# V of the first four token tiles from x as loaded, in a linear attention and SwiGLU kernel on Trainium2

## The chip, the cores and the metric

The kernel runs on one core of one Trainium2 chip. A core has a matrix engine (TensorE, PE in the profile), a vector engine (VectorE, DVE), a scalar engine for activations (ScalarE, ACT), a general engine (GpSimd, POOL) and a queue engine (SyncE, SP) that issues the transfers between DRAM and the core's memory here. [...] Each engine takes its instructions in the order of the program and waits on semaphores. The metric is the device time of one launch, in microseconds (us).

## What is computed

The input x has 2048 tokens of 640 numbers. It is normalised per token (mean and variance, no weights) to xn, and two branches of xn are added to x: a linear attention of 32 heads with a Hedgehog feature map, and a SwiGLU block with 1536 hidden columns.

```python
xn = _layernorm(x, axis=-1)
# A: q, k, v = split(xn @ wqkv), 32 heads of 20
pq = einsum("bhsd,hdf->bhsf", q, w_phi); pk = einsum("bhsd,hdf->bhsf", k, w_phi)
phi_q = concat([softmax(pq), softmax(-pq)]); phi_k = concat([softmax(pk), softmax(-pk)])
kv = einsum("bhsf,bhsd->bhfd", phi_k, v); z = einsum("bhsf->bhf", phi_k)
o = einsum("bhqf,bhfd->bhqd", phi_q, kv) / (einsum("bhqf,bhf->bhq", phi_q, z) + 1e-6)
a = o.reshape(B, S, D) @ wo
# B
b = (silu(xn @ w1) * (xn @ w3)) @ w2
return x + a + b
```

## The kernel before

The tokens are cut into 16 tiles of 128. `xin` holds x tiles as loaded (three buffers of four tiles, inside `reg_h`), `xnT` the normalised tiles transposed, `wv` the V weights (a third of `reg_w`), `wkT` and `wqT` the transposed K and Q weights (the other two thirds). The program is written out by hand in the order that each engine is to follow (`manual_schedule`), so a line's place in the code is its place in its engine's queue.

- **Loads.** SP issues all transfers (`ld`, L117; `ldT`, L130; transposes of `xnT`, L278). First x tiles 0 and 1, `wv` in three pieces (row blocks 0, 1 to 2, 3 to 4), x tiles 2 and 3. Two small POOL copies (L644, L649) hold the next loads back: columns 0 to 256 of w1 and w3, then x tiles 4 to 11, columns 256 to 512 of w1 and w3, and w_phi. x tiles 12 to 15 go to the buffer of tiles 0 to 3 (L677).
- **Warming.** 44 matmuls of zeros (`WARM`, `warm`, L193) run on PE while the first tile is loaded and normalised.
- **Normalising.** Per tile: statistics on DVE (`ln_stats`, L214 and L217), the root on ACT for tiles 0 to 3 (`ln_root`, L233), reciprocal and normalisation in place on DVE (`lx`, L616 and L268). For tiles 4 to 15 the inverse root is made on POOL (`stats`, L225 to L253).
- **Transposing.** `x_transposed` (called `T`) brings a normalised tile into `xnT`: tiles 0 to 3 by five PE transposes into PSUM (L282) and two ACT copies (L286), tiles 4 to 15 (`BY_DMA = 4`) by a DMA transpose (L278).
- **V and GLU at the start.** `V(t)` multiplies a transposed tile with `wv` (`by_token`, L304, ten matmuls of 360 and 280 columns) and ACT casts the result into `vaug` (`v_copy`, L319). GLU work comes in 48 units of 512 tokens by 128 hidden columns (`glu_unit`, L404); the first unit is done in two halves of 256 tokens (`glu_half`, L422). The order on PE is V of tiles 0 and 1, half a unit, V of tiles 2 and 3, the other half, units g1, g2, g3, V(4), V(5), and so on.
- **K stage** (L737): for each tile in the order 0 to 15, `phi_unit` makes the feature map (ten matmuls, six ACT exponentials, a DVE sum and reciprocal, a POOL product); two steps later `kv_unit` adds the tile into the accumulator `acc`; GLU units (`fill`) stand between, with the fusing of w_phi into the Q weights in steps 4 to 8.
- **Q stage and output** (L753): the same feature map for Q, the quotient, the output products. `If(ok == 0)` at the end is a path for large values which these inputs do not take.

Of the kernel before, what the change touches and what calls it, by code (L numbers as in the profile page):

```python
# [8 lines left out]
P = 128  # L9
# [3 lines left out]
def kernel(  # L13
# [32 lines left out]
    BY_ACT = (12, 13)  # L46
    WARM = 44

# [20 lines left out]
    def bank(name, dt=f32):  # L69
        n = 512 if dt == f32 else 1024  # L70
        return psum.tile([P, n], dt, name=name, tag="bank")

    def pair(name):
# [25 lines left out]
        "p (n c s) -> p n c s", n=2, c=NCH  # L99
    )  # L100
    vaug = reg_v[:, 0 : NST * NCH * VC].rearrange("p (t c e) -> p t c e", t=NST, e=VC)
    w2 = reg_v[:, 0 : KF * D].rearrange("p (c d) -> p c d", c=KF)
# [9 lines left out]
    state = slot(3)[:, 0 : 2 * (NCH * VC - Dh)].bitcast(f32)  # L112
    wide = one.tile([P, H * 21], f32, name="wide")


# [11 lines left out]
    with tc.manual_schedule():  # L127
# [14 lines left out]
        def ld_wv(c, n):  # L142
            src = A_wqkv[c * P : (c + n) * P, 2 * D : 3 * D]
            ld(wv[:, c : c + n], src.rearrange("(c p) f -> p c f", p=P))

        ld_tiles(0, 1)
        ld_tiles(1, 1)
        ld_wv(0, 1)
        ld_wv(1, 2)
        ld_wv(3, 2)  # L150
        ld_tiles(2, 1)
# [120 lines left out]

        def x_transposed(*ts, between=None):

            for t in ts:
                xn = xin[:, (t // 4) % 3, t % 4, :]
                if t >= BY_DMA:
                    nc.sync.dma_start_transpose(out=xnT[:, :, t * P : (t + 1) * P], in_=xn)  # L278
                    continue
                ps = bank("pst", bf)  # L280
                for c in range(KD):
                    nc.tensor.transpose(  # L282
                        ps[:, c * P : (c + 1) * P], xn[:, c * P : (c + 1) * P], ident[:]
                    )
                for c0, c1 in ((0, 2), (2, KD)):
                    nc.scalar.copy(  # L286
                        out=xnT[:, c0:c1, t * P : (t + 1) * P],
                        in_=ps[:, c0 * P : c1 * P].rearrange("p (c s) -> p c s", s=P),
                    )
                    if c0 == 0 and between:  # L290
                        between()

# [347 lines left out]


        ln_stats(0)
        ln_root(0)
        nc.gpsimd.tensor_copy(out=w1[0:1, 0, 0:1], in_=ry[0:1, 0:1])  # L644
        ld_glu(0, 256)
        ln_stats(1, between=lambda: lx(0, 1))
        T(0, between=lambda: ln_root(1))
        warm(4)
        nc.gpsimd.tensor_copy(out=xin[0:1, 1, 0, 0:1], in_=ry[0:1, 1:2])  # L649
        ld_tiles(4, 2)  # L650
        ld_tiles(6, 2)
        ld_tiles(8, 2)
        ld_tiles(10, 2)
        ld_glu(256, 512)
        ld(wps[:], A_w_phi.rearrange("h j f -> (h j) f").rearrange("(c p) f -> p c f", p=P))
        lx(1, 1)
        ln_stats(2)

        def second():
            T(1)  # L660
            ln_root(2)

        V(0, between=(4, second))
        ln_stats(3, between=lambda: lx(2, 1))
        pieces = list(chunks(by_token(tile_of(1), wv, "pv", CH)))
        v_copy(vaug[:, 1], *pieces[0])
        ln_root(3)


        first = (*glu.pop(0), *two("g0"))  # L670
        glu_half(0, *first, between=lambda: T(2))
        for piece in pieces[1:]:
            v_copy(vaug[:, 1], *piece)
        lx(3, 1)
        V(2, between=(3, lambda: T(3)))
        nc.scalar.activation(out=table[:], in_=nought[:, 0:1], func=AF.Tanh)
        ld_tiles(12, 4)  # L677
        ldT(wkT, 1, 0)
        pieces = list(chunks(by_token(tile_of(3), wv, "pv", CH)))
        stats(4, 2)  # L680
        stats(6, 2)
        glu_half(1, *first)
        g0 = glu_done(*first)
        for piece in pieces:
            v_copy(vaug[:, 3], *piece)
        lx(4, 2)
        T(4, 5)
        g1 = unit()
        g0()
# [30 lines left out]
        V(9)  # L720
        g5 = unit()
        lx(13, 1)
# [3 lines left out]
        phi_blocks()  # L726
        g5()
        lx(14, 2)
        T(14, 15)
        ldT(wkT, 1, 4)  # L730
        V(11)
        ld_glu(512, F)
        nc.sync.dma_start_transpose(out=wqT, in_=A_wqkv[:, 0:D])
        V(12), FB(0), FB(1), V(13), FB(2), V(14), FB(3), V(15), FB(4)


        acc = pair("pkv")  # L737
        for t in range(NST):
            phi_unit(t, wkphi, "pk")
            if t > 1:  # L740
                kv_unit(t - 2, vaug[:, t - 2], acc, t == 2, False)
            if t:
                fill(1)
            if 4 <= t < 9:
                fuse(wqphi, wqT, t - 4, [bank("pf"), bank("pf")])
            fill(1)
            if t >= 12:
                norm_unit(wkphi, 0, t - 12)
        ld(wo, A_wo.rearrange("(c p) d -> p c d", p=P))
# [3 lines left out]
        for t in range(NST + 4):  # L753
            if t < NST:
                phi_unit(t, wqphi, "pq")
            if t < 2:
                kv_unit(NST - 2 + t, vaug[:, NST - 2 + t], acc, False, t == 1)
                if t == 1:
                    kv_done([acc[:, 0], acc[:, 1]])
                    ld(w2, B_w2.rearrange("(c p) d -> p c d", p=P))  # L760
# [76 lines left out]
```

## Time and profile before

| | value |
|---|---|
| median of three runs | 270.03 us (269.9, 270.03, 270.25) |
| span of the profiled execution | 268.6 us, 5257 instructions |
| PE busy | 263.1 us, 98% |
| DVE busy | 188.7 us, 70% |
| ACT busy | 111.6 us, 42% |
| POOL busy | 95.6 us, 36% |
| DMA moved | 27.81 MB, mean 104 GB/s |

The span runs from the first to the last instruction of one profiled execution; the median of the timed runs is 1.4 us above it. In the rows that follow, a line of the timeline gives start and duration in us, the engine, the line of the kernel, the operation, output and inputs by the program's names, shapes and the number of instructions merged; in brackets stand the idle time before it and what ended it. `reg_h` is where `xin` lies, `reg_w` where the V, K and Q weights lie, `reg_v` where `vaug` lies, `pst` are the PSUM tiles of transposes. PE's matmuls are pipelined, and the end of each is modelled.

### The profile page before, as it was taken

To read this page: it belongs to the slowest core of one execution; us is meant where nothing else is said; L and a number is where in the kernel's file an instruction comes from. 1 tells how busy PE (TensorE), PEld (TensorE's weight loads), DVE (VectorE), ACT (ScalarE), POOL (GpSimd) and SP (SyncE) were. 2 spreads that over 40 slices of the span, in tenths; PEclk is the share of its full clock that TensorE was granted. 3 is DMA by queue.
4 is the path that set the end of the run, shared out by engine and by line. 5 is a ranking of instruction groups with operands and counts; after the bars stand their busy time and mean duration, and the time that the engine had idled before them with its cause. 6 is when DMAs were issued, how large, how long until landed. Compare 5 with 4: busy or idle time off the path is not lost.

```text
span 268.6 us, 5257 instructions
## 1 busy us (share of the span) xinstructions
PE 263.1 (98%) x1979; PEld 167.9 (63%) x1996; DVE 188.7 (70%) x348; ACT 111.6 (42%) x342; POOL 95.6 (36%) x99
## 2 busy tenths in 40 slices
PE   8999999999999999999999999999999999999995
PEld 8656667555555555555555445677777777777773
DVE  4899950887776667777777788876766777776341
ACT  2673668544555554346656545422222222221000
POOL 5054740354433333334444321333344444433000
PEclk9999999999999999999999999999999999999999
DMA  6998347970000000000000874355556655556831
GB/s 213 324 219 147 84 100 208 278 200 2 0 0 2 0 4 0 0 4 0 0 2 0 240 164 99 75 136 128 130 133 125 151 128 128 129 144 136 155 98 55
DMA packets 62909, 27.81 MB, mean 104 GB/s; under 512 B 49952, under 2 KB 61600, under 8 KB 62880
## 3 DMA queue, kind: packets, MB, share of 16 engines
q1 hardware_dynamic: 62880, 27.43, 42.2%
q8 instruction: 17, 0.28, 0.4%
q14 instruction: 12, 0.10, 0.1%
HBM read 12.81 MB, written 2.62 MB: 57 GB/s over the span
## 4 chain that ended last, share of the span: by engine, by line
PE 97%; ACT 1%; issue 0%; DVE 0%
PE acc L547 28%; PE up L404 19%; PE gp L404 18%; PE pv L304 8%; PE pq L304 8%; PE pk L304 8%; PE pr L484 2%; PE pkv L449 2%; PE idle L193 2%; PE pf L388 1%; PE g L422 1%; PE g L404 1%; PE pst L282 1%; ACT reg_v L319 0%; ACT xnT L286 0%
## 5 line engine op out<-in xcount | busy, mean ns | idle before, releaser
L370 POOL TENSOR_TENSOR phi<-phi,rk 128x1320 bf16<-128x1320 bf16 x32 | 77.3, 2415 | 133.4 <-DVE rk L369 94.8
L367 DVE TENSOR_REDUCE sk<-phi 128x66 f32<-128x1320 bf16 x32 | 48.9, 1528 | 40.8 <-ACT phi L333 39.7
L404 PEld LDWEIGHTS <-w 128*128 128x128 bf16 x470 | 44.6, 98 | 49.4
L304 PEld LDWEIGHTS <-xnT 128*128 128x128 bf16 x480 | 45.3, 98 | 21.6 <-ACT xnT L286 1.6
L404 PE MATMUL up<-xnT,w 128*128 128x512 bf16 x227 | 57.0, 379 | 0.3
L404 PE MATMUL gp<-xnT,w 128*128 128x512 bf16 x216 | 55.9, 378 | 0.6
L547 PE MATMUL acc<-reg_v,reg_h 128*128 128x320 bf16 (+2 forms) x384 | 54.9, 299 | 0.0
L333 ACT ACTIVATE phi<-pq 128x360 bf16<-128x360 f32 (+2 forms) x96 | 24.8, 364 | 58.0 <-issue 44.1
L547 PEld LDWEIGHTS <-reg_h 128*128 128x128 bf16 x384 | 37.3, 98 | 14.4
L415 ACT ACTIVATE th<-gp 128x512 f32<-128x512 f32 x46 | 27.7, 603 | 30.2 <-PE gp L404 29.7
L439 DVE SCALAR_TENSOR_TENSOR reg_h<-gs,up 128x512 bf16<-128x512 bf16 x46 | 31.7, 688 | 5.1 <-PE pk L304 0.5
L333 ACT ACTIVATE phi<-pk 128x360 bf16<-128x360 f32 (+2 forms) x96 | 24.8, 364 | 24.1 <-PE pk L304 24.1
L436 DVE SCALAR_TENSOR_TENSOR gs<-th,gp 128x512 bf16<-128x512 f32 x46 | 30.2, 658 | 0.0
L556 DVE TENSOR_TENSOR res<-acc,xr 128x320 bf16<-128x320 f32 (+2 forms) x32 | 14.3, 487 | 20.3 <-PE acc L547 20.3
L304 PE MATMUL pk<-wkphi,xnT 128*128 128x360 bf16 (+1 forms) x160 | 24.5, 299 | 0.0
L547 PE MATMUL acc<-reg_w,reg_v 128*128 128x320 bf16 (+2 forms) x160 | 24.5, 299 | 0.0
L304 PE MATMUL pq<-wqphi,xnT 128*128 128x360 bf16 (+1 forms) x160 | 24.3, 299 | 0.0
L304 PE MATMUL pv<-reg_w,xnT 128*128 128x360 bf16 (+1 forms) x160 | 23.7, 300 | 0.4 <-ACT xnT L286 0.4
L369 DVE RECIPROCAL rk<-sk 128x66 f32<-128x66 f32 x32 | 18.1, 566 | 3.2
L547 PEld LDWEIGHTS <-reg_v 128*128 128x128 bf16 x160 | 15.7, 98 | 6.1
L319 ACT CAST reg_v<-pv 128x360 bf16<-128x360 f32 (+2 forms) x48 | 13.3, 354 | 6.5 <-PE pv L304 6.3
L214 DVE BATCH_NORM_STATS2 st<-reg_h 128x6 f32<-128x320 bf16 x32 | 13.9, 470 | 2.0 <-DMA reg_h<-in_A_x_dram 2.0
(72 smaller groups left out, 145.6 us busy)
## 6 DMA issues: line engine op xcount, KB each, us to landing
w<-in_B_w_dram SPq DMA_DIRECT2D x2, 1280.0 KB, 8.7
xr<-in_A_x_dram SPq DMA_DIRECT2D x16, 160.0 KB, 2.5
out_dram<-res SPq DMA_DIRECT2D x15, 160.0 KB, 1.8
reg_v<-in_B_w_dram SPq DMA_DIRECT2D x1, 1920.0 KB, 9.1
w<-in_B_w_dram SPq DMA_DIRECT2D x4, 320.0 KB, 5.6
reg_h<-in_A_x_dram SPq DMA_DIRECT2D x4, 320.0 KB, 4.7
reg_w<-in_A_wo_dram SPq DMA_DIRECT2D x1, 800.0 KB, 4.6
reg_h<-in_A_x_dram SPq DMA_DIRECT2D x4, 160.0 KB, 3.6
```

What stands on the lines that cost most here:

```text
L214: nc.vector.bn_stats(out=st[:, i, :], in_=xt[:, i * HD : (i + 1) * HD])
L304: nc.tensor.matmul(ps[i][:, 0 : b - a], xnT[:, c, cols], w[:, c, a:b], start=(c == 0), stop=(c == KD - 1), skip_group_check=True,)
L333: nc.scalar.activation(out=dst[:, c0 : c0 + n, g, 0:k], in_=p.rearrange("p (c f) -> p c f", c=n), func=AF.Exp, scale=1.0 - 2.0 * g,)
L367: nc.vector.reduce_sum(out=sk[:], in_=rows, axis=AX.X)
L369: nc.vector.reciprocal(out=rk[:], in_=sk[:])
L370: nc.gpsimd.tensor_mul(out=rows, in0=rows, in1=rk[:, :, :, None].to_broadcast([P, 2 * NCH, 3, Dh]))
L404: nc.tensor.matmul(ps, w[:, c, fi * P : (fi + 1) * P], xnT[:, c, sc * 512 : (sc + 1) * 512], start=(c == 0), stop=(c == KD - 1),)
L415: nc.scalar.activation(out=th[:], in_=gp, func=AF.Tanh, scale=0.5)
L436: nc.vector.scalar_tensor_tensor(out=gs[:], in0=th[:], scalar=1.0, in1=gp, op0=ALU.add, op1=ALU.mult)
L439: nc.vector.scalar_tensor_tensor(out=hT[:, 4 * sc : 4 * sc + 4, fi, :], in0=gs[:].rearrange("p (t s) -> p t s", t=4), scalar=0.5, in1=up.r ...
L547: nc.tensor.matmul(ps[:, 0 : b - a], rows[j][0], rows[j][1][:, a:b], start=(j == 0), stop=(j == len(rows) - 1),)
L556: nc.vector.tensor_tensor(out=res[:, a:b], in0=ps[:, 0 : b - a], in1=xr[:, a:b], op=ALU.add)
```

## The change

V of token tiles 0 to 3 (`RAW = 4`) is no longer made from normalised x. The tiles are transposed as loaded into `xrT` (which lies in `wqT`'s place), multiplied with `wv` (`raw_part`), and scaled by the inverse deviation while ACT takes the result out of PSUM (`raw_scaled`, into `v_raw`, fp32). What is then too much in V is the mean times the inverse deviation times the column sum of `wv`. These column sums are made in the K stage: `wv` is loaded once more, transposed, into `wkT`'s place, ACT sums its rows with a factor -1 (`column_sum`), the sums go through DRAM and come back on all partitions (`less_sum`), and DVE adds them times `drift` into `vaug` (`raw_centred`). So that `vaug` of tiles 0 to 3 is ready when it is read, K takes the tiles in the order 4 to 15, then 0 to 3 (`turns`).

Normalised x of tiles 0 to 3 is still needed, by GLU and by K and Q. Tiles 0 and 1 are transposed by PE a second time after they are normalised; tiles 2 and 3 are transposed by DMA, where PE did it before. `wv` comes in five pieces. The load of w1 and w3 is no longer held back by POOL, and stands after the first scaled eviction in the code. The loads of columns 256 to 512 of w1 and w3, of x tiles 8 to 11 and of w_phi stand behind the two new DMA transposes on SP. The warming takes 19 matmuls of zeros in place of 44. Two GLU units are cut in halves in place of one, and the unit g5 stands after V(11).

```diff
@@ -44,7 +44,8 @@
     SAFE = 36.0
     BY_DMA = 4
     BY_ACT = (12, 13)
-    WARM = 44
+    WARM = 19
+    RAW = 4
 
 
     NCH = 11
@@ -98,6 +99,7 @@
     phiqT = reg_w[:, KD * D : KD * D + 2 * NCH * P].rearrange(
         "p (n c s) -> p n c s", n=2, c=NCH
     )
+    xrT = reg_w[:, KD * D : KD * D + KD * RAW * P].rearrange("p (c s) -> p c s", c=KD)
     vaug = reg_v[:, 0 : NST * NCH * VC].rearrange("p (t c e) -> p t c e", t=NST, e=VC)
     w2 = reg_v[:, 0 : KF * D].rearrange("p (c d) -> p c d", c=KF)
     oT = reg_v[:, KF * D : KF * D + KD * 512].rearrange("p (c s) -> p c s", c=KD)
@@ -111,6 +113,13 @@
     v_one = slot(2)[:, 0 : NCH * VC].rearrange("p (c e) -> p c e", e=VC)
     state = slot(3)[:, 0 : 2 * (NCH * VC - Dh)].bitcast(f32)
     wide = one.tile([P, H * 21], f32, name="wide")
+
+    v_raw = one.tile([P, RAW, D], f32, name="v_raw")
+    less_sum = wide[:, 0:D]
+    sums = one.tile([P, KD], f32, name="sums")
+    drift = one.tile([P, RAW], f32, name="drift")
+    dram = ctx.enter_context(tc.tile_pool(name="dram", bufs=1, space=bass.MemoryType.DRAM))
+    row = dram.tile([KD, P], f32, name="row")
 
 
     def ld(dst, src):
@@ -145,9 +154,8 @@
 
         ld_tiles(0, 1)
         ld_tiles(1, 1)
-        ld_wv(0, 1)
-        ld_wv(1, 2)
-        ld_wv(3, 2)
+        for c in range(KD):
+            ld_wv(c, 1)
         ld_tiles(2, 1)
         ld_tiles(3, 1)
 
@@ -270,25 +278,63 @@
                 op0=ALU.subtract, op1=ALU.mult,
             )
 
-        def x_transposed(*ts, between=None):
+        def x_transposed(*ts):
 
             for t in ts:
                 xn = xin[:, (t // 4) % 3, t % 4, :]
                 if t >= BY_DMA:
                     nc.sync.dma_start_transpose(out=xnT[:, :, t * P : (t + 1) * P], in_=xn)
                     continue
-                ps = bank("pst", bf)
-                for c in range(KD):
-                    nc.tensor.transpose(
-                        ps[:, c * P : (c + 1) * P], xn[:, c * P : (c + 1) * P], ident[:]
-                    )
-                for c0, c1 in ((0, 2), (2, KD)):
-                    nc.scalar.copy(
-                        out=xnT[:, c0:c1, t * P : (t + 1) * P],
-                        in_=ps[:, c0 * P : c1 * P].rearrange("p (c s) -> p c s", s=P),
-                    )
-                    if c0 == 0 and between:
-                        between()
+                by_pe(xnT, t)
+
+        def by_pe(dst, t):
+            xt = xin[:, (t // 4) % 3, t % 4, :]
+            ps = bank("pst", bf)
+            for c in range(KD):
+                nc.tensor.transpose(
+                    ps[:, c * P : (c + 1) * P], xt[:, c * P : (c + 1) * P], ident[:]
+                )
+            for c0, c1 in ((0, 2), (2, KD)):
+                nc.scalar.copy(
+                    out=dst[:, c0:c1, t * P : (t + 1) * P],
+                    in_=ps[:, c0 * P : c1 * P].rearrange("p (c s) -> p c s", s=P),
+                )
+
+        def raw_part(t, c, ps):
+            for i, (a, b) in enumerate(((0, CH), (CH, D))):
+                nc.tensor.matmul(
+                    ps[i][:, 0 : b - a],
+                    xrT[:, c, t * P : (t + 1) * P],
+                    wv[:, c, a:b],
+                    start=(c == 0),
+                    stop=(c == KD - 1),
+                    skip_group_check=True,
+                )
+
+        def raw_scaled(t, ps):
+            for i, (a, b) in enumerate(((0, CH), (CH, D))):
+                nc.scalar.activation(
+                    out=v_raw[:, t, a:b], in_=ps[i][:, 0 : b - a],
+                    func=AF.Identity, scale=rstd[:, t : t + 1],
+                )
+
+        def column_sum(c):
+            junk = work.tile([P, D], bf, name="junk")
+            nc.scalar.activation(
+                out=junk[:], in_=wkT[:, c], func=AF.Identity, scale=-1.0,
+                accum_out=sums[:, c : c + 1],
+            )
+
+        def raw_centred(t):
+            for c0, n, k in ((0, 10, 60), (10, 1, 40)):
+                cols = slice(60 * c0, 60 * c0 + k * n)
+                nc.vector.scalar_tensor_tensor(
+                    out=vaug[:, t, c0 : c0 + n, 1 : 1 + k],
+                    in0=less_sum[:, cols].rearrange("p (c e) -> p c e", c=n),
+                    scalar=drift[:, t : t + 1],
+                    in1=v_raw[:, t, cols].rearrange("p (c e) -> p c e", c=n),
+                    op0=ALU.mult, op1=ALU.add,
+                )
 
         def tile_of(t):
             return slice(t * P, (t + 1) * P)
@@ -639,53 +685,66 @@
             fuse(wkphi, wkT, d, ps)
 
 
+        by_pe(xrT, 0)
+        warm(4)
         ln_stats(0)
         ln_root(0)
-        nc.gpsimd.tensor_copy(out=w1[0:1, 0, 0:1], in_=ry[0:1, 0:1])
+        by_pe(xrT, 1)
+        ln_stats(1)
+        ln_root(1)
+        vps = [two("v0")] + [[bank("pv"), bank("pv")]]
+        lx(0, 1)
+        for c in range(2):
+            raw_part(0, c, vps[0])
+            raw_part(1, c, vps[1])
+        T(0)
+        raw_part(0, 2, vps[0])
+        raw_part(1, 2, vps[1])
+        lx(1, 1)
+        T(1)
+        raw_part(0, 3, vps[0])
+        raw_part(1, 3, vps[1])
+        raw_part(0, 4, vps[0])
+        by_pe(xrT, 2)
+        raw_part(1, 4, vps[1])
+        by_pe(xrT, 3)
+        raw_scaled(0, vps[0])
         ld_glu(0, 256)
-        ln_stats(1, between=lambda: lx(0, 1))
-        T(0, between=lambda: ln_root(1))
-        warm(4)
         nc.gpsimd.tensor_copy(out=xin[0:1, 1, 0, 0:1], in_=ry[0:1, 1:2])
         ld_tiles(4, 2)
         ld_tiles(6, 2)
+        ln_stats(2)
+        ln_root(2)
+        ln_stats(3)
+        ln_root(3)
+        raw_scaled(1, vps[1])
+        lx(2, 1)
+        nc.sync.dma_start_transpose(out=xnT[:, :, tile_of(2)], in_=xin[:, 0, 2, :])
+        lx(3, 1)
+        nc.sync.dma_start_transpose(out=xnT[:, :, tile_of(3)], in_=xin[:, 0, 3, :])
+        ld_glu(256, 512)
+        for t in (2, 3):
+            ps = [bank("pv"), bank("pv")]
+            for c in range(KD):
+                raw_part(t, c, ps)
+            raw_scaled(t, ps)
+        nc.scalar.activation(out=table[:], in_=nought[:, 0:1], func=AF.Tanh)
+        nc.gpsimd.tensor_mul(out=drift[:], in0=mv[:, 0:RAW, 0], in1=rstd[:, 0:RAW])
         ld_tiles(8, 2)
         ld_tiles(10, 2)
-        ld_glu(256, 512)
         ld(wps[:], A_w_phi.rearrange("h j f -> (h j) f").rearrange("(c p) f -> p c f", p=P))
-        lx(1, 1)
-        ln_stats(2)
-
-        def second():
-            T(1)
-            ln_root(2)
-
-        V(0, between=(4, second))
-        ln_stats(3, between=lambda: lx(2, 1))
-        pieces = list(chunks(by_token(tile_of(1), wv, "pv", CH)))
-        v_copy(vaug[:, 1], *pieces[0])
-        ln_root(3)
-
-
-        first = (*glu.pop(0), *two("g0"))
-        glu_half(0, *first, between=lambda: T(2))
-        for piece in pieces[1:]:
-            v_copy(vaug[:, 1], *piece)
-        lx(3, 1)
-        V(2, between=(3, lambda: T(3)))
-        nc.scalar.activation(out=table[:], in_=nought[:, 0:1], func=AF.Tanh)
         ld_tiles(12, 4)
         ldT(wkT, 1, 0)
-        pieces = list(chunks(by_token(tile_of(3), wv, "pv", CH)))
+        first = [(*glu.pop(0), *two("g0")), (*glu.pop(0), bank("gp")[:], bank("up")[:])]
+        for g in first:
+            glu_half(0, *g)
         stats(4, 2)
         stats(6, 2)
-        glu_half(1, *first)
-        g0 = glu_done(*first)
-        for piece in pieces:
-            v_copy(vaug[:, 3], *piece)
+        for g in first:
+            glu_half(1, *g)
+        g0, g1 = [glu_done(*g) for g in first]
         lx(4, 2)
         T(4, 5)
-        g1 = unit()
         g0()
         lx(6, 2)
         T(6, 7)
@@ -718,34 +777,44 @@
         lx(12, 1)
         T(12)
         V(9)
-        g5 = unit()
         lx(13, 1)
         T(13)
         ldT(wkT, 1, 3)
         V(10)
         phi_blocks()
-        g5()
         lx(14, 2)
         T(14, 15)
         ldT(wkT, 1, 4)
         V(11)
+        g5 = unit()
+        g5()
         ld_glu(512, F)
         nc.sync.dma_start_transpose(out=wqT, in_=A_wqkv[:, 0:D])
         V(12), FB(0), FB(1), V(13), FB(2), V(14), FB(3), V(15), FB(4)
 
 
+        turns = [*range(RAW, NST), *range(RAW)]
         acc = pair("pkv")
-        for t in range(NST):
+        for i, t in enumerate(turns):
             phi_unit(t, wkphi, "pk")
-            if t > 1:
-                kv_unit(t - 2, vaug[:, t - 2], acc, t == 2, False)
-            if t:
+            if i > 1:
+                kv_unit(turns[i - 2], vaug[:, turns[i - 2]], acc, i == 2, False)
+            if i:
                 fill(1)
-            if 4 <= t < 9:
-                fuse(wqphi, wqT, t - 4, [bank("pf"), bank("pf")])
+            if 4 <= i < 9:
+                fuse(wqphi, wqT, i - 4, [bank("pf"), bank("pf")])
             fill(1)
-            if t >= 12:
-                norm_unit(wkphi, 0, t - 12)
+            if i == 0:
+                nc.sync.dma_start_transpose(out=wkT, in_=A_wqkv[:, 2 * D : 3 * D])
+            if 4 <= i < 9:
+                column_sum(i - 4)
+            if i == 9:
+                ld(row[:].rearrange("c p -> p c"), sums[:])
+                ld(less_sum, row[:].rearrange("c p -> (c p)").partition_broadcast(P))
+            if 10 <= i < 10 + RAW:
+                raw_centred(i - 10)
+            if i >= 12:
+                norm_unit(wkphi, 0, i - 12)
         ld(wo, A_wo.rearrange("(c p) d -> p c d", p=P))
 
 
@@ -754,7 +823,7 @@
             if t < NST:
                 phi_unit(t, wqphi, "pq")
             if t < 2:
-                kv_unit(NST - 2 + t, vaug[:, NST - 2 + t], acc, False, t == 1)
+                kv_unit(turns[t - 2], vaug[:, turns[t - 2]], acc, False, t == 1)
                 if t == 1:
                     kv_done([acc[:, 0], acc[:, 1]])
                     ld(w2, B_w2.rearrange("(c p) d -> p c d", p=P))
```

## The prediction

> **What bounds the kernel now.** First the page, its chain of waits. It says that TensorE (PE) work fills the span nearly end to end, so only idle time of PE, or PE work without use, can be won or lost.
>
> ```profile
> PE 97%; ACT 1%; issue 0%; DVE 0%
> ```
>
> Second the timeline of PE up to the second batch of V, since the edit sits there.
>
> ```profile
> 1.05 4.87 PE L193 MATMUL idle<-nought 128*128 128x128 bf16 x44 [1.05 <-DVE nought L189]
> 5.72 0.73 PE L282 MATMUL pst<-ident,reg_h 128*128 128x128 bf16 x5
> 6.25 0.42 PE L193 MATMUL idle<-nought 128*128 128x128 bf16 x4
> 6.91 1.28 PE L304 MATMUL pv<-reg_w,xnT 128*128 128x360 bf16 x8 [0.24 <-ACT xnT L286]
> ...
> 16.17 1.03 PE L404 MATMUL gp<-xnT,w 128*128 128x512 bf16 x4
> ...
> 20.27 2.32 PE L404 MATMUL g<-xnT,w 128*128 128x512 bf16 x10
> 22.43 1.79 PE L304 MATMUL pv<-reg_w,xnT 128*128 128x360 bf16 x12
> ```
>
> PE multiplies zeros until tile 0 is normalised: the first useful transpose is at 5.72. From there it hardly stops. The last row is V(4); that moment, 22.43, is what I follow, because PE is packed from it to the end. The 44 idle matmuls start 106 ns apart; from 6.34 the spacing is 56 ns, so the clock doubles there.
>
> Third the queue of SyncE (SP) in the same stretch, with duration of the issue, not of the transfer.
>
> ```profile
> 7.32 1.91 SPq L117 DMA_DIRECT2D reg_h<-in_A_x_dram  x4
> 9.27 1.04 SPq L117 DMA_DIRECT2D w<-in_B_w_dram  x2
> 10.35 0.60 SPq L117 DMA_DIRECT2D wps<-in_A_w_phi_dram  x1
> 13.06 1.14 SPq L117 DMA_DIRECT2D reg_h<-in_A_x_dram  x1
> 14.24 1.97 SPq L130 DMA_TRANSPOSE reg_w<-in_A_wqkv_dram  x1
> 16.59 5.70 SPq L278 DMA_TRANSPOSE xnT<-reg_h  x4
> 22.34 1.27 SPq L130 DMA_TRANSPOSE reg_w<-in_A_wqkv_dram  x1
> ```
>
> SP issues every load in order: about 0.5 a copy, 1.23 a transpose (the tile's instructions). From 13 on it has little slack. Fourth the DMA issues of the window 12 to 17, last column us to landing.
>
> ```profile
> reg_h<-in_A_x_dram SPq DMA_DIRECT2D x1, 640.0 KB, 6.7
> reg_w<-in_A_wqkv_dram SPq DMA_TRANSPOSE x1, 6.3
> xnT<-reg_h SPq DMA_TRANSPOSE x1, 4.5
> ```
>
> Transposed tile 4, which V(4) reads, landed at 16.59+4.5=21.1, 1.3 before V(4). That is all the slack there is.
>
> **The change, part by part.**
>
> *Earlier start on PE.* 25 idle matmuls go (25 x 0.106 = 2.65); tiles 0 to 3 get a raw transpose and tiles 0 and 1 a second one, so six sets of five against four: +10 transposes, 0.28 a set on the fast clock, 0.56 in all. PE now reaches useful work at 1.05+19x0.106=3.07; x tile 0 landed at 0.80+2.2=3.0. Tile 1 landed at 1.27+2.8=4.1, the first chunk of wv at 1.72+2.8=4.5; the others are now five issues and not three, with the same bytes ahead: as before the last by about 7.1, x tiles 2 and 3 at 7.6 and 8.0 (3.18+4.4, 3.69+4.3). Laid end to end (a V chunk pair 0.53 on the slow clock, 0.27 on the fast one, the clock doubling at 6.34 as before): tile 1's transposes end at 4.7, three chunk pairs and a wait for ACT's copy bring 6.4, six pairs and two transposed tiles 8.6, raw tiles 2 and 3 with a pair between them 9.4. V of tiles 2 and 3 is ten pairs, 2.7 us: 12.3. The first halves of two GLU units, 4 x 0.55 (10 in 1.09, from the 14.86 group): 14.4.
>
> *The second halves need tiles 2 and 3 normalised and transposed.* These transposes leave PE and become DMA issues. Their chain: ACT makes eight copies out of PSUM in program order (tiles 0 and 1 normalised, 2 and 3 raw), 0.75 a tile by the row at 8.51; they begin at about 7.2, after tile 0's normalised transposes, wait a little for PE between, and end at 10.4. Two scaled evictions of tile 0 follow (three casts took 0.82; two wider ones 0.7), then the root for tile 2 (0.3): 11.3. Reciprocal 0.16 and normalisation 0.45 on DVE: 11.95. So SP, which stands at tile 2's transpose since about 7.4, issues it at 12.0 and tile 3's at 13.3 (1.23+0.05 each), and is free at 14.5. With an empty queue a transpose landed 2.4 after its issue (the one at 30.4): tile 3 at 15.65. PE waits from 14.4 to 15.65, does both second halves by 17.85 and two more units of 4 x 1.08 by 22.2. It would be 0.2 early at V(4).
>
> *What stands behind that wait on SP.* w1 and w3 columns 256 to 512, x tiles 8 to 11, w_phi, x tiles 12 to 15, wk block 0 and the transposes of tiles 4 to 7 are all queued there. Before, the four 320 KB copies and w_phi were out by 10.95; now they go from 14.5 to 17.2 (4 x 0.51 + 0.65). w1 and w3 land by about 17 and 18, in time for 17.85. x 12 to 15 is issued at 17.2 in place of 13.06, 4.1 later. From that issue to tile 4's landing took 21.1-13.06=8.0. Carried over, tile 4 lands at 25.2. Built from pieces: copies ahead done by 20.2 (from 17, about 1.0 per 320 KB, as 7.98 to 11.57 gave for four), 2.0 for 640 KB, 1.4 to 1.8 for wk, 0.6 for the transpose: 24.2 to 24.6. I take 24.8, so V(4) starts 24.85 against 22.43: **+2.4**. Bounds: 23.0 if only wk's own time counts (the transpose behind wk's next block landed 4.6 after that block's issue; 18.4+4.6), +0.65; 25.3, +2.9. Tiles 5 to 7 follow some 0.6 apart while a V takes 1.36, and tile 8 lands near 29 with V(8) starting no sooner than 34.9, so nothing more is late.
>
> Of this transpose I use the 1.23 that SP spent. [...]
>
> *K stage.* Tiles 4 to 15 first changes no count. Added: one 11 us transposed load of wv into wkT's place, two small DMAs, five column sums on ACT (0.93 by the 128x640 row at L263, plus 0.19 for the accumulator: 5.6), eight DVE operations (0.66 for 512 columns, so some 0.8 and 0.2: 4.0 for the four tiles). V loses one cast a tile. Between 48 and 100 PE idles 0.3 of 52 while ACT is busy 26 and DVE 40; a step is some 6.2 long, so ACT has 3 and DVE 1.4 free in each and the extra is 1.1 or 1.0 per step. SP has nothing else there, and the sums have two steps to come back from DRAM. I take 0; with the cover gone DVE's 4.0 would show; I allow 0.3. On the other side nothing of K gets cheaper.
>
> *Sum.* -0.2 at V(4) without the late tile, +2.6 for waiting: +2.4 on the profiled execution's span of 268.6, so 271.0. Around it lie 1.4 (the median of the three runs is 270.03), the same after: **272.4**.
>
> **Rivals.**
>
> *A lighter queue.* Copies behind the wait find an empty DMA and tile 4 lands at 23.0 to 24: 270.7 to 271.6. For it: before, the load of x 12 to 15 waited among others. Against: DMA share was 1.0 in the window 12 to 17.
>
> [...]
>
> *The other side: the queue is no queue.* Each transpose lands 2.4 after its own issue, whatever is ahead, as those at 30.4 and 33.1 did. Tile 4, issued at 19.7, lands at 22.1, before PE comes at 22.2: 269.8. If ACT's copies also finish as early as the landing of x tile 3 allows (SP goes on at 11.0), every step is 1.0 earlier and PE too: 268.8. It decides when tile 4 lands before 22.4. Against: the transpose at 16.59 took 4.5, the one at 23.7 took 3.2.
>
> *It does what it says and nothing is late.* Halves at 14.4 without a wait, V(4) at 20.9: 268.5. This needs tile 3 by 14.4, with its issue before 12.0.
>
> *The K stage pays.* Column sums and centring push PE: up to 4.0 more, 273 to 276. Against: the idle shares above.
>
> **How the numbers follow.** Forecast (tile 4 at 24.2 to 25.3): 0.50. Lighter queue 0.16, late clock 0.14, other side 0.11, nothing late 0.04, K pays 0.05. The range runs from 269.6, which holds most of the other side's 269.8, to 274.4 above the late clock; about 0.15 is left out. The forecast's own range is 271.7 to 273.0. A change under 0.2% (0.5 us) cannot be told from none: faster 0.12 (other side and nothing late, less what stays within 0.5), same 0.07, slower 0.81.
>
> **What would show it.** Right: PE's raw transposes from 3.1; SP silent from about 7.4 to 12, then two transposes; PE idle some 1.2 before the second GLU halves and some 2.6 before V(4), both released by a DMA of xnT; spacing of 56 ns from about 6.3; K steps as long as before. Wrong: V(4) at or before 22.4, or those gaps without a DMA as releaser, or K longer.

## The result, and the profile after

The changed kernel takes 274.52 us (median of five runs, 272.88 to 274.8), the kernel before in the same comparison 269.9 us (269.69 to 270.25): 4.6 us between the medians. The ratio of the runs side by side is 1.0154, 95% interval 1.0128 to 1.018, or 4.2 us: slower. The profiled execution of the changed kernel is its quickest of the five, 272.88 us with a span of 271.2, against a span of 268.6 before: 2.6 us longer.

First the chain of waits of the changed kernel, as shares of the span by engine.

```profile
PE 87%; DVE 4%; DMA 4%; POOL 1%; SPq 1%; issue 1%; ACT 1%; DVEq 0%
```

Before, PE had 97% of the chain. Transfers and SP's issuing (SPq) are on it now, with DVE and POOL. The timeline of PE in the changed kernel tells where; its columns are those of the prediction's.

```profile
1.05 2.21 PE L201 MATMUL idle<-nought 128*128 128x128 bf16 x19 [1.05 <-DVE nought L197]
3.11 0.71 PE L294 MATMUL pst<-ident,reg_h 128*128 128x128 bf16 x5
...
4.90 0.43 PE L305 MATMUL v<-reg_w 128*128 128x360 bf16 x2 [0.44 <-DMA reg_w<-in_A_wqkv_dram]
...
8.81 2.89 PE L305 MATMUL pv<-reg_w 128*128 128x360 bf16 x20
...
13.18 0.71 PE L468 MATMUL up<-xnT,w 128*128 128x256 bf16 x5
15.46 1.27 PE L468 MATMUL g<-xnT,w 128*128 128x256 bf16 x10 [1.57 <-DMA xnT<-reg_h]
...
20.11 2.32 PE L450 MATMUL g<-xnT,w 128*128 128x512 bf16 x10
24.33 5.61 PE L350 MATMUL pv<-reg_w,xnT 128*128 128x360 bf16 x40 [1.90 <-DMA xnT<-reg_h]
...
35.02 3.21 PE L350 MATMUL pv<-reg_w,xnT 128*128 128x360 bf16 x20 [0.21 <-DMA xnT<-reg_h]
...
47.24 1.72 PE L350 MATMUL pk<-wkphi,xnT 128*128 128x360 bf16 x10
```

Useful work starts 2.6 us earlier (3.11 against 5.72), and PE then gives that back, and more, above all at two waits for DMA transposes: 1.57 us ahead of the second GLU halves (tile 3) and 1.90 us ahead of V(4) (tile 4). V(4) starts at 24.33 against 22.43. A third, small one stands at V(10): 0.21 us, and inside the row 3.21 us for twenty matmuls that take 2.88 where nothing is late. K starts at 47.24; before:

```profile
44.62 1.72 PE L304 MATMUL pk<-wkphi,xnT 128*128 128x360 bf16 x10
```

So the loss is 2.62 at the start of K, of which 1.90 is there at V(4) and 0.72 comes between. From the start of K to the end of the span it is 223.94 us in both: nothing is lost or won behind 47.24. In each of the profiles below for which a start of K is given it is 223.94 to 223.99, so there too the start of K tells the whole difference.

Next the queue of SP in the changed kernel, start and duration of the issue.

```profile
6.16 1.54 SPq L126 DMA_DIRECT2D reg_h<-in_A_x_dram  x2
11.60 1.33 SPq L722 DMA_TRANSPOSE xnT<-reg_h  x1
13.05 1.20 SPq L724 DMA_TRANSPOSE xnT<-reg_h  x1
14.30 1.14 SPq L126 DMA_DIRECT2D w<-in_B_w_dram  x2
...
17.20 0.40 SPq L126 DMA_DIRECT2D reg_h<-in_A_x_dram  x1
17.65 2.66 SPq L139 DMA_TRANSPOSE reg_w<-in_A_wqkv_dram  x1
20.35 5.24 SPq L286 DMA_TRANSPOSE xnT<-reg_h  x4
```

SP issues nothing from 7.70 to 11.60: it stands at tile 2's transpose until DVE has normalised that tile (11.12 to 11.57). x tiles 12 to 15 leave at 17.20 (before: 13.06), and tile 4's transpose at 20.35 (before: 16.59). The DMA issues of the stretch 17 to 21.6, last column us from issue to landing:

```profile
reg_h<-in_A_x_dram SPq DMA_DIRECT2D x1, 640.0 KB, 5.8
reg_w<-in_A_wqkv_dram SPq DMA_TRANSPOSE x1, 6.1
xnT<-reg_h SPq DMA_TRANSPOSE x1, 3.9
```

20.35 + 3.9 = 24.25: tile 4 lands there and V(4) starts at 24.33.

Last, the K stage, as busy time in equal stretches of 94.9 us, between K's first matmul and Q's first: PE, PE's weight loads, DVE, ACT, POOL (instructions in brackets), granted clock, DMA share, GB/s. The kernel before:

```profile
44.70:139.60 94.90, 94.22 (x644) 52.02 (x654) 70.53 (x92) 49.78 (x149) 36.70 (x16) 1.00 0.16 44
```

The changed kernel:

```profile
47.30:142.20 94.90, 94.86 (x656) 52.04 (x654) 73.95 (x99) 53.35 (x159) 36.65 (x16) 1.00 0.21 51
```

DVE does 3.4 us more and ACT 3.6, and both still leave over 20 us idle; PE stays full and the stage keeps its length.

### The profile page after: what moved, and what is told of

It reads as the page before. It is cut to its first block, busy times and chain, and to the rows that moved or that the text cites. A ratio compares the mean times of both kernels' runs of the same rounds, so it can differ in the third digit from the quotient of the medians.

```text
span 271.2 us, 5298 instructions
## 1 busy us (share of the span) xinstructions
PE 262.6 (97%) x1991; PEld 166.6 (61%) x1991; DVE 192.1 (71%) x356; ACT 116.7 (43%) x352; POOL 95.5 (35%) x99
## 3 DMA queue, kind: packets, MB, share of 16 engines
HBM read 13.13 MB, written 2.62 MB: 58 GB/s over the span
## 4 chain that ended last, share of the span: by engine, by line
PE 87%; DVE 4%; DMA 4%; POOL 1%; SPq 1%; issue 1%; ACT 1%; DVEq 0%
PE acc L593 27%; PE gp L450 17%; PE up L450 17%; PE pq L350 8%; PE pk L350 8%; PE pv L350 3%; DVE st L222 2%; PE pr L530 2%; PE pkv L495 2%; DMA reg_h<-in_A_x_dram 2%; PE pv L305 2%; DMA reg_w<-in_A_wqkv_dram 1%; PE pf L434 1%; DMA xnT<-reg_h 1%; SPq L126 1%
## 5 line engine op out<-in xcount | busy, mean ns | idle before, releaser
L450 PEld LDWEIGHTS <-w 128*128 128x128 bf16 x460 | 43.5, 97 | 48.6 <-DMA w<-in_B_w_dram 0.6
L450 PE MATMUL up<-xnT,w 128*128 128x512 bf16 x225 | 55.9, 379 | 0.0
L350 PEld LDWEIGHTS <-xnT 128*128 128x128 bf16 x440 | 41.6, 98 | 22.1 <-DMA xnT<-reg_h 3.4
L602 DVE TENSOR_TENSOR res<-acc,xr 128x320 bf16<-128x320 f32 (+2 forms) x32 | 14.3, 486 | 20.0 <-PE acc L593 20.0
L350 PE MATMUL pv<-reg_w,xnT 128*128 128x360 bf16 x120 | 17.6, 299 | 2.2 <-DMA xnT<-reg_h 2.1
L551 DVE TENSOR_TENSOR o__77<-pr,den 128x360 bf16<-128x360 f32 (+1 forms) x32 | 14.2, 486 | 0.6
```

Source lines behind the costliest of these rows:

```text
L350: nc.tensor.matmul(ps[i][:, 0 : b - a], xnT[:, c, cols], w[:, c, a:b], start=(c == 0), stop=(c == KD - 1), skip_group_check=True,)
L450: nc.tensor.matmul(ps, w[:, c, fi * P : (fi + 1) * P], xnT[:, c, sc * 512 : (sc + 1) * 512], start=(c == 0), stop=(c == KD - 1),)
L602: nc.vector.tensor_tensor(out=res[:, a:b], in0=ps[:, 0 : b - a], in1=xr[:, a:b], op=ALU.add)
```

## The experiments

Edits are against the changed kernel unless another is named. Each ratio is against the kernel before, run beside it.

**The changed kernel again, and the other places for the loads.** Three kernels and a repeat were to tell the queue (what stands in line ahead of tile 4) from the transfers, and the 0.72 us behind V(4) from both.

*The changed kernel once more.*

> The changed kernel once more, for a second profile. Its five times lay 1.9 us apart (272.88 to 274.8) and the profiled one was the fastest, with the matmul spacing falling from 106 to 56 ns at 4.0 us where the kernel before had it at 6.3. Clock theory: the moment of that fall moves from launch to launch; if it falls at 6 us or later here, the raw transposes of tiles 2 and 3 end up to 1 us later than 8.7, SP issues tile 2's transpose up to 1 us later than 11.6, V(4) starts at 24.8 to 25.8 and not at 24.33, and the time is 273.5 to 274.8. Rival (the DMA queue varies by itself): the spread is there with the clock falling at 4.0 again, and the landing of tile 4 moves against its issue by a microsecond or more.

273.71 us (273.27 to 274.01), ratio 1.0147 [1.0133, 1.0162]. In this profile V(4) starts at 24.93 and K at 47.55. The spacing of PE's matmuls fell from 106 to 56 ns at 3.73 us, so the launch does not hold the late clock that the expectation asks about, and does not decide on it. It does show that a launch with an early clock can still be 0.3 longer: tile 4's transpose left at 20.96, not 20.35, and took the same 3.9 us to land.

*x tiles 12 to 15 and wk behind the transposes of tiles 4 to 7.*

```diff
-        ld_tiles(12, 4)
-        ldT(wkT, 1, 0)
         first = ...
...
         T(6, 7)
+        ld_tiles(12, 4)
+        ldT(wkT, 1, 0)
```

> x tiles 12 to 15 and block 0 of the K weights are issued behind the transposes of tiles 4 to 7; nothing else changes. Queue theory (V(4) is late because 8 us of issues and transfers stand between SP's wait and tile 4): tile 4 lands at about 21.5 to 22.5, the wait before V(4) is under 0.3 us, V(4) starts at 21.7 to 22.6. Of the 2 us won there, some 1.2 is lost again at V(10), whose tile then is the late one because the GLU unit g5 stands behind V(11): total 0.5 to 1.2 us faster than the changed kernel. Rival (PE or the transfers themselves are the limit): tile 4 still lands after 23.5 and V(4) moves by less than 0.8.

274.44 us (273.42 to 276.74), ratio 1.0191 [1.0155, 1.0227]: no gain, where 0.5 to 1.2 us was expected. SP in this kernel:

```profile
17.53 7.23 SPq L286 DMA_TRANSPOSE xnT<-reg_h  x4
```

and PE:

```profile
23.60 5.71 PE L350 MATMUL pv<-reg_w,xnT 128*128 128x360 bf16 x40 [0.90 <-DMA xnT<-reg_h]
...
32.52 2.89 PE L350 MATMUL pv<-reg_w,xnT 128*128 128x360 bf16 x20 [1.04 <-DMA xnT<-reg_h]
36.96 2.91 PE L350 MATMUL pv<-reg_w,xnT 128*128 128x360 bf16 x20 [1.56 <-DMA xnT<-reg_h]
```

Tile 4's transpose is issued 2.8 earlier (17.53 against 20.35) but V(4) comes only 0.7 earlier, because the transpose now lands 6.0 us after its issue: the held-back copies are still in flight ahead of it (x tiles 8 to 11 land 5.9 us after their issue in this run). And x tiles 12 to 15 and wk, later now, push tiles 8 and 10 behind their V. The order on SP alone is not the limit; the transfers that SP could not start before 14.3 are. That is the rival's side of the expectation.

*The unit g5 back where it was.*

```diff
         V(9)
+        g5 = unit()
...
         phi_blocks()
+        g5()
...
         V(11)
-        g5 = unit()
-        g5()
```

> The GLU unit g5 is put back between V(9), V(10) and V(11), as in the kernel before; nothing else changes. Theory (0.7 us of the loss arises at V(10) and V(11), which come 2.2 us earlier against the transposes of tiles 10 and 11 since g5 moved): the waits before V(10) and V(11) go, the K stage starts 0.4 to 0.7 us earlier, 0.4 to 0.7 faster than the changed kernel. Rival (that 0.7 comes from the transposes of tiles 12 to 15 being late anyway): the waits move to V(13) or V(14) and the time stays within 0.2.

273.75 us (272.62 to 275.31), ratio 1.0157 [1.0127, 1.0186]. PE in this kernel:

```profile
25.12 5.61 PE L350 MATMUL pv<-reg_w,xnT 128*128 128x360 bf16 x40 [2.05 <-DMA xnT<-reg_h]
...
37.60 4.24 PE L350 MATMUL pv<-reg_w,xnT 128*128 128x360 bf16 x30
```

With the unit between V(9) and V(10) the row at 37.60 has no wait. From V(4) to the start of K it is 22.21 us (K at 47.33), as before the change (22.19), against 22.91 in the changed kernel. So the move of g5 uncovers the transposes of tiles 10 and 11, and that is the 0.72. The median (273.75 against 273.71) does not show it, since three of the six runs had a mean granted clock of 0.994 (274.4, 274.83, 275.31). The three at 1.00 took 272.62, 272.98 and 273.11, mean 272.90; the four runs of the changed kernel beside them, all at 1.00, average 273.68, some 0.8 more; the shift that was expected, 0.4 to 0.7, is met in these few runs only.

**Taking the two DMA transposes away.** *PE transposes tiles 2 and 3, between the first GLU halves.*

```diff
         lx(2, 1)
-        nc.sync.dma_start_transpose(out=xnT[:, :, tile_of(2)], in_=xin[:, 0, 2, :])
         lx(3, 1)
-        nc.sync.dma_start_transpose(out=xnT[:, :, tile_of(3)], in_=xin[:, 0, 3, :])
...
-        nc.scalar.activation(out=table[:], in_=nought[:, 0:1], func=AF.Tanh)
...
-        ld_tiles(12, 4)
-        ldT(wkT, 1, 0)
         first = ...
-        for g in first:
-            glu_half(0, *g)
+        glu_half(0, *first[0])
+        T(2)
+        T(3)
+        ld_tiles(12, 4)
+        ldT(wkT, 1, 0)
+        nc.scalar.activation(out=table[:], in_=nought[:, 0:1], func=AF.Tanh)
+        glu_half(0, *first[1])
```

> Normalised tiles 2 and 3 are transposed by PE again (ten transposes and four ACT copies, between the two first GLU halves), so SP has no transpose to wait for; the loads behind it go out at once. Queue theory: SP issues the copies of w1 and w3 from about 7.8 and x tiles 12 to 15 at about 14, tile 4 lands at 20 to 21.5, no wait before V(4), V(4) at 20.8 to 22; the gain of the early start shows there. Then V(10) waits up to 2 us for its tile: 0.7 to 1.5 us faster than the changed kernel in all, so still slower than the kernel before. Rival (two more transposes do no harm, the late tile has another cause): V(4) stays at 24.

271.5 us (271.14 to 271.89), ratio 1.006 [1.0048, 1.0072]: 2.2 faster than the changed kernel beside it, more than expected. PE:

```profile
21.82 5.89 PE L350 MATMUL pv<-reg_w,xnT 128*128 128x360 bf16 x40
...
34.21 2.89 PE L350 MATMUL pv<-reg_w,xnT 128*128 128x360 bf16 x20 [1.62 <-DMA xnT<-reg_h]
```

Both waits of the changed kernel are gone, and V(4) starts 0.6 before its old place. The earlier V(4) makes the wait at V(10) longer, 1.62, where g5 is missing.

*The same with g5 back* (both edits together).

> Both repairs together: normalised tiles 2 and 3 transposed by PE, and the unit g5 back before V(10) and V(11). Theory (two losses, one at V(4) by SP's wait, one at V(10) because its tile's normalisation on DVE is late against a PE that comes 2.2 us early): neither wait is left, the K stage starts at 44.3 to 45.0 against 46.1 with the first repair alone and 44.62 in the kernel before; 1.1 to 1.6 us faster than the first repair alone, within 0.4 us of the kernel before. Rival (DVE and the transposes are late for all tiles from 10 on): the wait moves to V(12) to V(14) and less than 0.5 us is won.

270.46 us (269.67 to 270.82, eleven runs), ratio 1.0012 [1.0003, 1.0021]: level with the kernel before, within the 0.2% that can be told. The row at V(10) has no wait, and K starts at 43.89 in the profiled launch, which is the quickest of the eleven:

```profile
21.06 5.89 PE L350 MATMUL pv<-reg_w,xnT 128*128 128x360 bf16 x40
...
33.90 4.28 PE L350 MATMUL pv<-reg_w,xnT 128*128 128x360 bf16 x30
...
43.89 1.72 PE L350 MATMUL pk<-wkphi,xnT 128*128 128x360 bf16 x10
```

So the DMA transposes and the place of g5 make up the slowdown but for 0.2 us. Of the 1.37 us by which V(4) is early here (21.06 against 22.43) 0.73 is left at K; the rest goes in pauses of 0.2 us and less. Why is the early start, then, not a gain? Two kernels on top of this one ask that.

*Warming off, and warming as long as before* (against the kernel with both edits; in the second kernel 44 stands in place of the 0).

```diff
-    WARM = 19
+    WARM = 0
```

> The same with no idle matmuls ahead of the first transposes (0 in place of 19; the four after them stay). Clock theory (the clock doubles only after PE has worked for most of one window of some 3.4 us): PE begins at 3.0, the spacing falls at 7 to 10 us and not at 4 to 6.5, raw V ends 0.8 to 1.7 us later and the time is 0.4 to 1.7 us longer than with both repairs. Rival (19 idle matmuls do nothing for the clock that the transposes do not): spacing falls by 6.5 and the time is within 0.3.

> Both repairs, but 44 idle matmuls as in the kernel before in place of 19, so that useful PE work begins at 5.7 and not 3.1. If the early start is worth what PE wins by it, this is 1.2 to 2.0 us slower than both repairs with 19. If it is swallowed by later waits on DVE and transposes, less than 0.5 slower.

Without the zeros: 271.4 us (271.1 to 271.89), ratio 1.0047 [1.0035, 1.0059]. The medians are 0.94 apart. In the two profiles the spacing of 56 ns comes at 7.28 in place of 3.76, and V(4) starts 1.18 later (22.24 against 21.06); the other launches' doublings were not seen, so the price of a late clock, an estimate from these two kernels, is about 1 us, no closer. PE's work begins at 3.19 there: of the 3.41 us that end at 7.28 it fills all, of the 3.41 before those 0.68. With 44 of them: 272.23 us (271.0 to 272.35), ratio 1.007 [1.0054, 1.0086], 1.77 longer. That is what the early start of PE is worth in the kernel with both edits. With 44 zeros that kernel is 272.23 - 270.25 = 2.0 slower than the kernel before beside it, which starts after 44 as well. So V from raw x, with the second transposes of tiles 0 and 1 and all that hangs on them, costs about 2.0 us ahead of K (K starts at 46.65 in its profile, 44.62 before) and gives back the 1.8.

**The queue turned round.** *The copies that waited behind the two transposes go ahead of them.*

```diff
         ld_tiles(6, 2)
+        ld_glu(256, 512)
+        ld_tiles(8, 2)
+        ld_tiles(10, 2)
+        ld(wps[:], A_w_phi.rearrange("h j f -> (h j) f").rearrange("(c p) f -> p c f", p=P))
         ln_stats(2)
...
-        ld_glu(256, 512)
...
-        ld_tiles(8, 2)
-        ld_tiles(10, 2)
-        ld(wps[:], ...)
```

> The changed kernel with the copies that stand behind the two DMA transposes on SP (w1 and w3 columns 256 to 512, x tiles 8 to 11, w_phi) moved ahead of them. SP does not hold them up any more, but the transposes then land behind 1.3 MB of copies. Queue and transfer theory: tiles 2 and 3 land at 16.5 to 18, PE waits 2.5 to 4 us before the second GLU halves in place of 1.6, x tiles 12 to 15 can go only after that, tile 4 lands at 22.5 to 25; the total within 1 us of the changed kernel. If SP's wait alone were the cause: no wait before V(4) over 0.3 us and 1.5 to 2.5 us faster.

275.5 us (274.88 to 275.79), ratio 1.0193 [1.0178, 1.0209]: slower still. Tiles 2 and 3 are now issued at 12.8 and 15.3, tile 3 lands behind the copies, and PE waits 4.50 us for it, more than the 2.5 to 4 expected:

```profile
18.75 1.92 PE L468 MATMUL g<-xnT,w 128*128 128x256 bf16 x10 [4.50 <-DMA xnT<-reg_h]
20.46 1.27 PE L468 MATMUL gp<-xnT,w 128*128 128x256 bf16 x5
```

Ten matmuls that took 1.27 in the changed kernel take 1.92, and five take 1.27 for 0.71. The busy times of four stretches, with the granted clock behind the engines' five columns:

```profile
14.00:19.20 5.20, 0.70 (x7) 0.41 (x5) 3.28 (x10) 1.38 (x2) 3.45 (x12) 1.00 0.92 180
19.20:22.60 3.40, 3.40 (x19) 2.42 (x17) 1.23 (x2) 1.19 (x2) 0.00 (x0) 0.50 0.68 205
22.60:26.00 3.40, 3.35 (x16) 1.57 (x16) 3.33 (x10) 0.60 (x1) 1.14 (x3) 1.00 0.91 198
15.80:19.20 3.40, 0.45 (x4) 0.41 (x5) 1.55 (x5) 0.00 (x0) 2.48 (x10) 1.00 0.77 99
```

After the wait the clock is halved for 3.41 us (19.21 to 22.62 in the trace's record of the clock), from 0.45 us after work has begun again. In this launch the spacing of PE's first matmuls fell to 56 ns at 5.55, and 5.55 + 4 x 3.41 = 19.2: the drop fits a count of windows of that length, of which the last, 15.8 to 19.2, holds 2.95 us of the wait and 0.45 of work. All four runs had a mean clock of 0.994, which is what such a stretch gives (1 - 0.5 x 3.4/274).

**The clock in the changed kernel.** Its profiled launch has no stretch like that ahead of the end, but two of its five runs had a mean clock of 0.992 and 0.994. The profile shows how near it came. Counted on from the doubling at 3.97 in windows of 3.413 us, the length that 78 of them need to the clock's fall at 270.21, after PE's last matmul (268.13), one window holds most of the wait before V(4):

```profile
21.04:24.45 3.41, 1.51 (x8) 0.54 (x7) 3.24 (x9) 0.60 (x1) 2.50 (x7) 1.00 1.17 271
266.80:270.21 3.41, 1.33 (x13) 0.95 (x10) 0.49 (x2) 0.00 (x0) 0.00 (x0) 1.00 0.18 53
270.21:271.10 0.89, 0.00 (x0) 0.00 (x0) 0.00 (x0) 0.00 (x0) 0.00 (x0) 0.50 0.09 28
```

The window with 1.51 us of PE's work kept the clock, the one with 1.33 lost it, as the one with 0.45 did where the copies were put first (ends of matmuls as modelled). So, as an estimate from these rows (3.41 - 1.51 and 3.41 - 1.33), a wait halves the clock in this kernel when it takes more than 1.9 to 2.1 us out of one window. The wait before V(4) took 1.75 to 2.35 us in the five profiles of this kernel, and a window's end can split it: by this estimate it is then a matter of the launch whether the clock falls. The 1.57 us ahead of the second halves is less than that; the window around it (14.21 to 17.62) holds 2.16 us of work and kept the clock.

*Multiplications of zeros in both waits, with the changed kernel as partner on the same chip.*

```diff
+        def busy(n):
+            ps = bank("busy")
+            for _ in range(n):
+                nc.tensor.matmul(ps[:, 0:P], nought[:], nought[:])
...
         stats(6, 2)
+        busy(26)
...
+        busy(36)
         V(4)
```

> The changed kernel a third time, as the partner of the next one on the same chip: 272.9 to 274.8, median near 273.9. In the profile the wait before the second GLU halves is 1.5 to 1.9 us, that before V(4) 1.8 to 2.8, the K stage begins at 47.0 to 48.5.

> The changed kernel with idle matmuls in its two waits: 26 before the second GLU halves, 36 before V(4) (1.5 and 2.0 us at 56 ns). They use no data, so PE stays busy while it waits and the real work begins when it did. Where copies were put first, a wait of 4.5 us on PE was followed by 3.4 us at half clock (19.2 to 22.6). Clock theory of the spread: in the slower launches of the changed kernel the two waits bring the clock down too; then this one is 0.6 to 1.5 us faster in the median than its partner and its times lie within 0.8 us of each other. Rival (waits of 1.6 and 2.3 us do not reach the clock; the spread comes from the landing of tile 4): same within 0.4 us and the same spread.

The partner: 274.76 us (272.8 to 275.24), ratio 1.017 [1.0156, 1.0184], later than the 273.9 expected; four of its six runs had a mean clock of 0.992 or 0.994. The filled kernel: 274.12 us (274.04 to 274.31), ratio 1.014 [1.0124, 1.0155], none of four below 0.998. PE in the filled kernel:

```profile
14.26 1.61 PE L683 MATMUL busy<-nought 128*128 128x128 bf16 x26
...
22.83 2.17 PE L683 MATMUL busy<-nought 128*128 128x128 bf16 x36
...
25.38 4.25 PE L350 MATMUL pv<-reg_w,xnT 128*128 128x360 bf16 x30 [0.38 <-DMA xnT<-reg_h]
```

The zeros cover most of the waits (0.38 us is left at V(4) and 0.90 at V(7)), none of the four runs has a low mean clock, and the spread is 0.27 us against 2.4. What is left is the waiting itself: V(4) comes no sooner, and the median lies 0.6 below the partner's but not below the full-clock runs of the changed kernel (273.8 on average).

*Two more launches of the changed kernel, to catch the halved clock in a profile.*

> The changed kernel once more, one look, to catch a launch with a lowered mean clock in a profile. Clock theory: if the mean granted clock of the profiled launch is 0.995 or lower, its slices show one stretch of about 3.4 us at 0.50 soon after one of PE's two waits (between 15 and 31 us), with the matmuls there at twice their distance, K starts at 47.8 or later and the span is 272.5 or more; if the mean clock is 0.998 or more there is no such stretch, K starts at 47.1 to 47.6 and the span is 271.0 to 272.0. Rival: the mean clock is lowered only at the start or at the end, and the longer launches are longer by later landings of tile 4 alone, so that no stretch at half clock lies between 9 us and the last 10 us.

> The same again, a second chance to profile such a launch; same numbers: with a mean clock of 0.995 or lower a stretch of about 3.4 us at 0.50 between 15 and 31 us and K at 47.8 or later (clock theory), or none there (rival); with 0.998 or more no stretch and K at 47.1 to 47.6.

273.42 and 274.25 us, both at a mean clock of 1.00, so neither holds the stretch, and the halved clock stays without a profile in this kernel. K starts at 47.77 and 48.49, later than the 47.1 to 47.6 expected at full clock. PE in the second:

```profile
24.89 5.61 PE L350 MATMUL pv<-reg_w,xnT 128*128 128x360 bf16 x40 [1.99 <-DMA xnT<-reg_h]
...
36.60 2.89 PE L350 MATMUL pv<-reg_w,xnT 128*128 128x360 bf16 x20 [1.23 <-DMA xnT<-reg_h]
...
48.49 0.70 PE L350 MATMUL pk<-wkphi,xnT 128*128 128x360 bf16 x4
```

K starts at 48.49, 1.25 later than in the first profile, and the span of 272.4 is 1.2 longer, at full clock: 0.56 by V(4), the rest at V(10). There tile 10's transpose left at 32.19, 0.57 later than in the first profile, and landed 4.4 us after that in place of 3.4: at 36.6, when V(10) starts. Over the five profiles of the changed kernel V(4) starts at 24.33 to 24.93 (mean 24.69), and from there to K pass 22.62 to 23.60 (mean 22.95), 0.4 to 1.4 above the 22.19 of before.

## Why the prediction was right and where it was not

Forecast were 272.4 us and slower; measured were 274.52 and slower, 0.1 above the range (by the ratio, on the 270.03 of before, 274.2 and just inside it). The sign, the main mechanism and its place were right; the size was too small by two terms that the sum had at nothing, and by a part that stays open. That the range comes so near is luck: it reached to 274.4 for the late clock, which did not happen; the forecast's own 271.7 to 273.0 was missed.

*Earlier start on PE.* Right: 3.11 for 3.07, the raw chain done at 11.54 for 12.3. The difference is the clock, taken as doubling at 6.34 and doubling at 3.97 in this launch; in the fourth profile, with the doubling at 6.40, the chain is done at 12.22. It bought nothing, since the next step waits for SP.

*Second halves.* Right: SP stood silent to 11.60 (12.0 forecast), was free at 14.25 (14.5), tile 3 landed at about 15.45 (15.65), and PE waited 1.57 us for it (1.25 forecast; it came 0.5 earlier). The two issues held SP for 1.33 and 1.20 us (1.23 in the sum) where the five copies behind them took 0.47 to 0.57 each; in landing there is no such difference, 2.4 us for the second transpose (2.4 in the sum) against a median of 2.5 for the copies of 160 KB of `xr`.

*What stands behind that wait.* Right in mechanism and size: x tiles 12 to 15 issued at 17.20, as forecast, and V(4) at 24.33 to 24.93 over five profiles for 24.85, so +1.9 to +2.5 for +2.4. The order experiment and the copies moved ahead also bear out why: tile 4 is held by transfers that start late, not by its own issue, and putting them in front only holds tile 3.

*"So nothing more is late."* This step failed. It looked at tile 8 alone, and with a wrong row: 34.9 is not V(8) but V(10), as the kernel before shows.

```profile
30.02 2.88 PE L304 MATMUL pv<-reg_w,xnT 128*128 128x360 bf16 x20
...
34.89 4.24 PE L304 MATMUL pv<-reg_w,xnT 128*128 128x360 bf16 x30
```

The first row is V(8) and V(9), the second V(10) to V(12), with g5 between them. Before, tile 10's transpose left at 30.45 and landed 2.4 us later, 2.0 ahead of V(10). In the changed kernel it left at 31.62 and took 3.4, to 35.02, and PE, without g5's 2.16 us of cover, was there at 34.65. The sum had this at nothing; its price is 0.4 to 1.4 us, mean 0.75, and with g5 back in its place it is gone.

*The clock.* The late clock of the chances (0.14), for which the range reaches to 274.4, is a first doubling later than the 6.34 of before; no run shows the term behind that end of the range. What the runs show is a first doubling between 3.73 (`a_again`) and 6.52 (`pe_t`) in the profiled launches with 19 zeros, at most 0.2 past 6.34, and with the warming taken away one at 7.28, 3.5 later than the 3.76 of its partner, for about 1 us. What was missing in sum and rivals is that waits could bring the clock down again. That a wait of 4.50 us does is shown; that the changed kernel's wait before V(4) does in some launches is inferred from the rows of windows above, from mean clocks (6 of 17 runs at 0.992 to 0.994, where one halved window gives 1 - 0.5 x 3.41/272 = 0.994, and 0.992 together with the fall at the end, which left the first profile at 0.998; mean 274.8, the other eleven 273.8) and from the filled kernel. No launch with it was profiled.

By the profiles of two launches PE's transposes counted towards the doubling. Counted back from the first doubling in steps of 3.413 us, with 44 zeros (`late_start`) a window with 2.52 us of them (0.16 to 3.57) did not bring it, and in the second profile of the changed kernel (`a_again`) one with 2.68 us did (0.32 to 3.73), at most 2.33 of it zeros and the rest five transposes.

*K stage at nothing.* Right: 223.94 us from its start to the end in both kernels, so its rival fell too.

Put together at full clock: 2.26 at V(4) and 0.75 behind it are 3.0, and the five profiled launches average 273.32 against the 270.25 of the profiled launch before, 3.1 more. The six full-clock runs without a profile lie higher, at 273.5 to 274.7. The last of the five profiles (274.25) shows that later landings can do that, there of tile 10; which transpose it was in each of the six was not seen, and this part of the median stays open.

## What to carry to other kernels

A transfer that waits for a chain of compute, put on an in-order queue, delays everything behind it (here SP issued nothing from 7.70 to 11.60, and x tiles 12 to 15 left at 17.20 in place of 13.06): count what is queued there, and follow those transfers to their own readers, to the last one, before the move is called free. When a unit of independent work is moved, list every load whose cover it was. An earlier start is worth only what the first late operand lets through: here 1.8 us won at the front were paid by 2.0 of extra work, with the waits on top.

## What was not expected of the hardware

After PE had waited 4.50 us in the run with the copies first, its granted clock fell to 0.50 for 3.41 us, and it fell at 19.21, when work had already begun again (18.75). The falls stand at whole numbers of 3.413 us from the first doubling: there 4 (5.55 to 19.21), in the changed kernel 78 (3.97 to 270.21) and in the kernel before 77 (6.31 in the trace's record of the clock, to 269.14). In the changed kernel such a window kept the clock with 1.51 us of PE's work and lost it with 1.33. The spacing of PE's first matmuls dropped from 106 to 56 ns anywhere between 3.73 (`a_again`) and 7.28 us (`no_warm`), from launch to launch and kernel to kernel, while the granted clock in the profile's rows read 1.00 ahead of it too (0 to 4 us with the copies first, 1 to 6 us in the kernel before), so in these rows that column does not show the first doubling. A transpose of the same 128x640 tile landed 2.4 us after its issue with nothing ahead of it (tile 10 before), 3.9 in the changed kernel and 6.0 with copies in flight (both tile 4, the second in `sp_order`), and the issue of four of them held SP for 5.24 us in the changed kernel and for 7.23 behind those copies.
